# A gated linear recurrence and its MLP: decays of the states on ScalarE, block products for the last eight chunks, one mask operation per visit

## The chip, the cores and the metric

The kernel runs on one core of a Trainium2 chip. The metric is the device time of one execution in microseconds. Five engines with queues of their own work side by side: TensorE (PE in the profile; its weight loads are PEld), VectorE (DVE), ScalarE (ACT), GpSimd (POOL) and SyncE (SP), which issues the DMA transfers here. Every engine takes its instructions in order, so an instruction that waits holds up all behind it on that engine.

## What is computed

Four batches of eight heads run a recurrence over 768 tokens with a head width of 48. The state is a complex 48x48 matrix; each row is multiplied by a complex gate, whose magnitude is clipped at 0.999, and the outer product of key and value is added. The output of a token is the query times the real part of the new state. The heads' outputs form 3072 rows of 384, which run through an MLP: 384 to 2048 features, a leaky ReLU with a slope per feature, and back to 384.

```python
mag = np.sqrt(a_re * a_re + a_im * a_im)
scale = np.minimum(mag, 0.999) / (mag + 1e-06)
a_re_n, a_im_n = (a_re * scale, a_im * scale)
for t in range(S):
    ar, ai = (a_re_n[:, :, t, :, None], a_im_n[:, :, t, :, None])
    new_re = ar * S_re - ai * S_im
    new_im = ar * S_im + ai * S_re
    kv = np.einsum('bhd,bhe->bhde', k[:, :, t], v[:, :, t])
    S_re, S_im = (new_re + kv, new_im)
    y[:, :, t] = np.einsum('bhd,bhde->bhe', q[:, :, t], S_re)

x = np.ascontiguousarray(attn_out.transpose(0, 2, 1, 3)).reshape(B * S, H * D)
h = x @ w_in
g = np.maximum(h, 0.0) + alpha * np.minimum(h, 0.0)
return (g @ w_out).astype(np.float32)
```

## The kernel before, in words

The tokens are cut into 24 chunks of 128, six for each batch. A gate is split into a magnitude (the decay) and a rotation. The rotation is put into queries and keys, so that the state needs only real decays, one for each of the 96 rows (real and imaginary parts of 48) of each head.

**Gates** (`gates`, L223). A group of one or three chunks is worked through at once; the list `GATES` (L947) names the groups as (batch, first chunk, end). The large steps, over all tokens of a group, run on ScalarE and VectorE (L253 to L318, then L426 and L429 for the final rotations). Between them lies a long chain of dependent small steps that form running products of the rotations (`product`, L334 to L342; `three`, L363; L372 to L411). The names `tiny` and `small` decide which engine takes the small ones: VectorE in batch 0, GpSimd in the others (L232). The results go to DRAM (`decs`, `phs`) and are loaded back in another layout by `loads`, as PP and T. Two gate tiles are held at a time.

**Units** (`unit`, L637). One unit works a chunk through. L661 and L663 put the rotations on keys and queries. Then the positions inside the chunk are treated as a tree of six levels, 1, 2, 4, 8, 16 and 32, two levels in a "visit". For each level TensorE multiplies keys and queries (L678), the result in PSUM (`ps_lv`) is masked into a tile A of that level, and `step` (L717) multiplies queries and keys with the decays of that level on VectorE. Levels 1 to 8 are masked by VectorE, one operation each (L702), levels 16 and 32 by ScalarE (L699). Afterwards TensorE forms the chunk's own state terms (L797, tile `ps_kv`), the output from the levels (L817) and the output from the states before (L841), and the states go on: multiplied by the decay (L826) and added to (L829). The output is copied (L855) and goes through DRAM to become x of the MLP (`loads_x`).

**MLP** (`all_mlp`, L926). Groups of MLP rows are single chunks at both ends and pairs between (`sizes`). For each of the 16 blocks of 128 features, TensorE makes the features (`features`, L889: three matmuls into `ps_h`, two tiles of it), ScalarE and VectorE make the leaky ReLU (L896, L898), and `outputs` (L908) adds the block's product with w_out, 128 rows by 384 columns, to `ps_o`. After 16 blocks the sum is copied (L918) and sent. The output products of a group follow while the features of the next are made. The weights come in as 64-bit words and are turned into 32-bit floats at the start (`to_f32`: L507 to L511 on ScalarE, L515 on GpSimd, L517 and L519 on VectorE).

**Order.** Each of these routines is a generator; a `yield` stands ahead of each operation. The string `ORDER` names, letter by letter, which generator makes its next operation, and so fixes the order of the instructions on every engine and of the DMA issues. Waits follow from the data and the buffers: the `bufs` of each tile are what limits how far an engine may run ahead.

Of the kernel before, what the change touches and what calls it, by code (L numbers as in the profile page):

```python
# [9 lines left out]
F32 = mybir.dt.float32  # L10
# [8 lines left out]
P = 128  # L19
# [11 lines left out]
    "AABAMMAAAAAAAAAAAAAAAAAMAAAAAMABJMNAJNNABNAAAAAAAAAAAAANKJKAKBKNBAABAAAABABBJAAAALAAAAAAABAMAAAAOKAK"  # L31
    "AOBAAABMAAABAAABBBABLLBABAOMABAKBABABBBALNBNABABAABBOBAKBNBABBNOBNBOOOABBBOBMBBBNLONNBBBBBBOBLBBBOBN"
    "NOBBJBKJBNJBPBBBBBOBPBBPBBBPBCCBBOBKBPPPBNLBMPJCKBBCPLBLKKPBMBBOPKKOKBBCBPBCBPMBCBPBLPBNCLPLCPLBPBCP"
    "CLPCCCNPJJJCJONJNPCDCPPPPPPPPPPDPCPPCJMPCCPKPCPCQCQCNOCDPJCNCQCNLQCCPQJJCPCPQCDQPPNOPOCOQCOPJPCQPPPC"
    "DOQMCQNCQDLJQJnCQLQJCQCKKKLQDDQKOLCCKoQCKNONCQLLNCRCQNQCRQCQRNQDQQKCQMQODLCLRDQCRLNRRDDCLLORCQOLCQON"
    "ooCRCNCRLRMKOCCOCDONCJDQQMNDQCODNCRDCDRCCQNQOLCQCROCOMLRCLRMOCLODoDQJCLCCRQKRCCQCooLooLCLRQDLLLLLLCN"
    "QoRCDRDCDCoCKCCRCRCCCoRRRDoCKRRooRQCRCoCoooCJQQQRQooDRNoDoRRRQDJCRDRoNooooJooJoooRJoDoooORDooooooLLL"
    "LLLoooDODoDnoRDooRoOoERDRooNNRRLDoRoSRRoooNOoNooSoEooOoooNOSLOoSoNROSSoooSJDooSJJSJSLSJOooooooSSSooS"
    "SLSoDooELoLLSSooooooDSSLESoJSJoSSSSSooDooSSToDoooSDoSoETDEDTDoJoSSoSSJJSSEDoTSoooKJoTTooKooLDDoEoDoS"
    "LTKTToToDoDLSoLoDoTKoEEDTDSSoTTToSDDDLDoJLSoSSSooooSoDoDDEoooDToTToooDoEoLoooLDTnooDUoDLooEooooooEDo"  # L40
    "oEToTTDDDDDToToDJJJETJUooDoTDToooUoTTLLLEooLooooLToDUDETUTUUToETTTToUoDLDDoUDUDoUDTDoooooUooKDoKTLUo"
    "EUTUTTTEDDDLDoEEEoDoooooJJoDoTTKKoTToooELoooEDoooooTLUUDUULoLooLooLLoooooDoUDEUooEoETEoDooDoooooEooo"
    "LooLUUUUoEUUEoUEoLEEoooooUEUoEoUooEEooEUoooJoVUUUUJJUoJUEUVUUEoUUUUEEVJEEEFVoVooVoJoooooVVVoJUVUoooV"
    "oJFEoVVoJonoJooVWooVooWVVFoEFVLoooLoVEoLLLLLLVoooWLooooVoLWEEEEEEEEEEEEEEEoLooLoLoLKWoWVFJVEEVWJVVVo"
    "VooWooVVVoooVoWoVoKWWVoVJVVWoVVWWJEVVFEEEEEVEEJEEEWWVoLWooWoLoLLLLLEWLoEEXoFEKoLooEoWWWEFWXVWWFLWVEo"
    "LLVFLLooWVoooVVVVFJJJJEJoooWoooWEooWEWooWWWWEWEEWWEWWWEooWEWoLEXLWFoWFLoooLoXoLWoWoLoLoEoFooXXFXooFX"
    "oooooFELWLoLJXLJLoKoXXooLooFoooFoXoooooXXXFFXoooXXoXoooFFooFFXXoXLXXYooXFXFooXWJFXoXJooXnoXXYoYoooXX"
    "XooJJJoYFoFXFFoGXFXXFJLXXFYYFXFFXYXLXLXooGoLLLFXoooXooLJXooYoYLYFFoJJoooYoooGFoKYoFoFoooJYFFFYYZFGFo"
    "ZFFoFoYooJooYoYoooYooGooZoZFYYYYFYoFFFFYFJFJFFLoFooLoYoooYoJoLYYLooGoYLZLZYoooYoGYYYYFYFLZFLLZZGYFYY"
    "LFoYFZYYGYFLZFFFFFFZGFFFFFFaoYYoFoYoooooYYLLoZZZoLZoZnoLoZoooooooJFFLoLLLLZGJJJoJFoZFFFFZoKZGoZZFaFZ"  # L50
    "FooooooZZFZoKZoooFFooFooooZZooZZZZZZFZJZoZZGGZoZoZFooaZZZZooaGGaLoZGLoaaGJooLoooaaoLLLLaLJooJaJoLoaG"
    "ooooooLooooooaaooGabaooGooboooooaoGaboaLoHGHoGboooobGooboooGaaabaaaaGaabooKKGJoGaLLbbKoaoooaGGbboGoo"
    "GaoaaaaJaGaGoaKGaaHHaGaGaJGoGGGGoaGoJoaooaoKKooHoHHLooGcGoGoJbbGoGoocHoooooooLbboLLLGGGboJJJJobcoLoo"
    "oGooLoLGLocbbobooGGoooooocbcLLLbbbbbcnoboboHbGJcboobcoocooLLbbooobbcHGGbbbcbHoGoGGGGcLcGcGbGHLLLLobH"
    "HbGJHLLLGocobboobGLGGcGGGoccboooboooGoLGLGooHGoocccoGHocLdbdbbcocGoccGoJcGGooLLoocooHcGoHooGGoJKcGoJ"
    "JGGGGGGGHoooooocodcccccoHLLLLoLLoooLdooLoccGGGoHdoodooodLHdoIdoooooodJodoIoooooooLLLHHcocooooodLHooo"
    "oHooddccdooododHHdcodoJIoHHcHdddddddddHHHcoocoooKJccoHLooooooooodoooeJdHooJooondooddHHdHdHdJedoJdIdo"
    "dJddIddddoHooeoHodoJdHoooLedJJJeIeeeHeHoHooLeHoooLHIeooooooHJHeoooeLILeLHoLoLeooLIoLeeJfefofKooofHeo"
    "oooooLoooLoefefeofLeoooeIJeIILoeeooeoeHHHeHHHoHHHHHHHofeoJoIeoeeefeoefeeeIIefeeIJeooeoooIofeeooIeooo"
    "eoLLfffIfooHooooJofffIoIoooJLgJoggHLJHHHHHooooLLooooKHLoLoHoJLoLKLKLLLHgHHfggooIHHfooonffffoffHoooJf"  # L60
    "foHHofooKHHfoKfggHggoooIIIIoHooHoffffHfffffffHooLLHLHHLoLoooooHoHoIogHoooHoooIoIofHgooooooIoofIoIfLo"
    "HIIfLLLLLggggKoIoooooogJgooooIfoKgoooooLoggfgoLoohggIhggoooghogoIgoooJggoIohJooIJgggggggggJKgIIggJJI"
    "ghooIhLggoohohoLoogLJLohhoJhhooohhooooJooohhhioohIIoJoihoooIIooIihooiohnoooooooLIIILLohihihLhoohhhJo"
    "IhhoooLoohiJLLoLoLIIoiIIhIIIohIhILIioooIhhhhhhhhhLhJhoohIIIiiiIJIooLIIIoIhIIIIhhoojLhLooohooooooiiio"
    "iojLiooooJiJioJLLLojoIjoLoooLLLLLoooooooiIiIJIiijiIjiiiIooooIiiIoiooIjioIoooooIojIIIooIooooJioiiIjii"
    "ijoiiLiiLiLILiiiojoijooiIioLjiLjJIjILIoLoLojoooJoJjoooojoooooooJoooojoojjJojoojJoLooLoooookLoooojLko"
    "ookLojjjjokojoJkknJoJoookoojoookjoooojoooojjkkjjlojjokLkkkkjLLLLLLLLjLokooooookoookkoooooojokkkkkkkj"
# [933 lines left out]
```

## Time and profile before

The times of three runs are 837.02, 833.38 and 836.58 us, with a median of 836.58. The profiled execution took 836.36 us; its profile has a span of 834.6 us and a mean granted TensorE clock of 0.962.

| What | Busy us | Share of the span | Instructions |
|---|---|---|---|
| TensorE, matmuls | 695.8 | 83% | 11488 |
| VectorE | 651.7 | 78% | 1020 |
| ScalarE | 438.7 | 53% | 937 |
| GpSimd | 200.6 | 24% | 293 |

Every float32 matmul shows as two records, so a count of matmuls in the profile is halved for the number of instructions in the program. A group's row gives line, engine, operation, tile out <- tile in, shape out <- shape in and the count; then the busy time and the mean length in ns; then the idle time of the engine just before, and what ended it. A line of the timeline gives the start and the length in us. The row of slices gives each fortieth of the span as tenths of busy time. The "chain that ended last" follows the work back from the last instruction, always to what released it.

### The profile page before, as it was taken

What the parts mean: (1) busy time and instruction counts of PE and PEld (TensorE: products, weight loads), DVE (VectorE), ACT (ScalarE), POOL (GpSimd) and SP (SyncE); (2) the same over time, 40 slices, a digit from 0 to 9 for tenths busy, and PEclk for the clock granted to TensorE, in tenths of its full rate; (3) what the DMA queues carried; (4) which work ended last, traced back from release to release, by engine and by line L of the source; (5) the groups of instructions that cost most, each with busy time, mean ns of one, the idle gap of its engine ahead of it and who ended that gap; (6) DMA issues with size and microseconds to landing.
All of it is one profiled execution on the core that took longest, in us unless ns stands there. A gap on an engine that the chain in (4) does not pass through costs nothing.

```text
span 834.6 us, 26848 instructions
## 1 busy us (share of the span) xinstructions
PE 695.8 (83%) x11488; PEld 527.7 (63%) x11488; DVE 651.7 (78%) x1020; ACT 438.7 (53%) x937; POOL 200.6 (24%) x293
## 2 busy tenths in 40 slices
PE   0001435889998999899999999999999999999998
PEld 0001424667776777677777777777777777777776
DVE  5989999999997899889988988979767652644112
ACT  7758787467635665565657446644344342323221
POOL 5231222328603600360135103330341000000000
PEclk9999755899999999999999999999999999999999
DMA  6696977786478579737873586457834832511110
GB/s 195 189 280 157 274 170 227 217 220 175 100 222 209 145 171 248 186 88 197 233 194 77 158 259 159 115 143 216 210 99 118 202 70 61 136 34 43 35 30 10
DMA packets 194174, 130.91 MB, mean 157 GB/s; under 512 B 74120, under 2 KB 185864, under 8 KB 194056
## 3 DMA queue, kind: packets, MB, share of 16 engines
q1 hardware_dynamic: 194056, 129.20, 58.8%
q8 instruction: 90, 1.47, 0.7%
q14 instruction: 28, 0.23, 0.1%
HBM read 100.82 MB, written 35.71 MB: 164 GB/s over the span
## 4 chain that ended last, share of the span: by engine, by line
PE 53%; DVE 23%; DMA 12%; POOL 4%; issue 4%; ACT 4%; SPq 1%; DVEq 0%; ACTq 0%; POOLq 0%
PE ps_o L908 22%; PE ps_h L889 20%; DVE KQ L717 4%; DMA T<-decs 4%; PE ps_lv L678 4%; DVE gate L426 3%; DVE gate L338 2%; PE ps_y L817 2%; DMA phs<-gate 2%; PE ps_y L841 2%; PE ps_kv L797 2%; DVE gate L429 2%; DMA g_sb<-in_w_out_dram 1%; POOL gate L338 1%; DVE gate L340 1%
## 5 line engine op out<-in xcount | busy, mean ns | idle before, releaser
L889 PE MATMUL ps_h<-xT,w_in_sb 128*128 128x256 f32 (+1 forms) x1344 | 297.3, 355 | 9.0 <-DMA xT<-ysc 7.0
L908 PE MATMUL ps_o<-w_out_sb,g_sb 128*128 128x384 f32 x768 | 297.2, 500 | 7.9 <-DVE g_sb L898 4.5
L889 PEld LDWEIGHTS ps_h<-xT,w_in_sb 128*128 128x128 f32 x1344 | 235.7, 194 | 82.1 <-DMA xT<-ysc 7.8
L898 DVE SCALAR_TENSOR_TENSOR g_sb<-g_sb,al,ps_h 128x256 f32<-128x256 f32 (+1 forms) x224 | 97.5, 436 | 117.9 <-ACT g_sb L896 117.6
L896 ACT ACTIVATE g_sb<-ps_h 128x256 f32<-128x256 f32 (+1 forms) x224 | 78.8, 352 | 200.7 <-PE ps_h L889 199.4
L908 PEld LDWEIGHTS ps_o<-w_out_sb,g_sb 128*128 128x128 f32 x768 | 136.5, 191 | 59.4 <-DVE g_sb L898 7.0
L717 DVE TENSOR_TENSOR KQ<-KQ,T 96x1024 f32<-96x1024 f32 x120 | 149.2, 1246 | 23.8 <-PE ps_lv L678 15.2
L678 PE MATMUL ps_lv<-WQ 96*32 96x32 f32 x2304 | 34.3, 204 | 72.6 <-DVE WQ L661 56.2
L678 PEld LDWEIGHTS ps_lv<-WQ 96*32 96x32 f32 x2304 | 26.5, 116 | 92.7 <-DVE WQ L661 56.2
L740 ACT COPY WQ<-KQ 96x1024 f32<-96x1024 f32 x48 | 49.9, 1040 | 22.2 <-DVE KQ L717 22.2
L338 POOL TENSOR_TENSOR gate<-gate 128x72 f32<-128x72 f32 x42 | 25.8, 615 | 134.3 <-ACT gate L368 131.5
L515 POOL TENSOR_SCALAR top<-top 128x768 f32<-128x768 f32 x16 | 41.2, 2578 | 65.2 <-ACT top L507 65.1
L756 ACT COPY W<-KQ 96x512 f32<-96x512 f32 x48 | 30.9, 644 | 40.1 <-DVE KQ L717 30.3
L338 DVE TENSOR_TENSOR gate<-gate 128x576 f32<-128x576 f32 (+5 forms) x84 | 48.6, 579 | 3.8 <-ACT gate L368 2.4
L855 ACT COPY T<-ps_y 48x256 f32<-48x256 f32 x96 | 31.6, 365 | 34.5 <-PE ps_y L841 33.7
L817 PE MATMUL ps_y<-A,VL 64*48 64x64 f32 x2304 | 42.0, 224 | 4.4 <-issue 3.8
L426 DVE TENSOR_TENSOR gate<-gate 128x1152 f32<-128x1152 f32 (+2 forms) x36 | 43.6, 1235 | 0.1
L817 PEld LDWEIGHTS ps_y<-A,VL 64*48 64x48 f32 x2304 | 39.7, 125 | 5.4 <-issue 4.5
L699 ACT ACTIVATE A<-ps_lv,columns 128x64 f32<-128x64 f32 x144 | 37.6, 334 | 9.2 <-PE ps_lv L678 9.1
L678 PE MATMUL ps_lv<-KQ,W 96*32 96x32 f32 x1536 | 24.5, 203 | 20.3 <-ACT W L756 19.7
L702 DVE TENSOR_TENSOR A<-ps_lv,mask 128x256 f32<-128x256 f32 x96 | 37.6, 412 | 0.0
L717 DVE TENSOR_TENSOR KQ<-WQ,T 96x1024 f32<-96x1024 f32 x24 | 29.5, 1231 | 6.4 <-DMA T<-decs 4.2
(106 smaller groups left out, 899.4 us busy)
## 6 DMA issues: line engine op xcount, KB each, us to landing
T<-decs SPq DMA_DIRECT2D x48, 384.0 KB
PP<-phs SPq DMA_DIRECT2D x24, 387.0 KB
KQ<-in_q_dram SPq DMA_DIRECT2D x48, 192.0 KB
decs<-gate SPq DMA_DIRECT2D x7, 1152.0 KB
phs<-gate SPq DMA_DIRECT2D x14, 576.0 KB
KQ<-in_k_dram SPq DMA_DIRECT2D x40, 192.0 KB
vsc<-in_v_dram SPq DMA_DIRECT2D x48, 144.0 KB
VL<-vsc SPq DMA_DIRECT2D x24, 288.0 KB
```

Source lines behind the costliest of these rows:

```text
L338: on(4 * k).tensor_tensor(out=m, in0=w[:, 1::-1].unsqueeze(2).to_broadcast([P, 2, 2, k]), in1=pairs_of(u), op=ALU.mult)
L426: TT(out=m[:, a], in0=U5[:, 1 + a], in1=turned(off3, o)[:, a].unsqueeze(1).unsqueeze(3).to_broadcast([P, L // 2, nb, 2]), op=ALU.mult)
L515: nc.gpsimd.tensor_scalar(out=top, in0=top, scalar1=F64_SMALL, scalar2=None, op0=ALU.max)
L678: nc.tensor.matmul(t[64 * i + j:64 * i + j + HC // 2, p], lhsT=keys(n, g), rhs=queries(n, g), start=True, stop=True)
L699: nc.scalar.activation(a[:, :, cols], t[:, :, at:at + name], AF.Copy, scale=s)
L717: nc.vector.tensor_tensor(out=x, in0=x if x0 is None else x0, in1=m, op=ALU.mult)
L740: nc.scalar.copy(z.rearrange("p i n t -> p i (n t)").rearrange("p i (m h) -> p m i h", h=h), bass.AP(tensor=KQ.tensor, offset=KQ.offset + ...
L817: nc.tensor.matmul(o, lhsT=Vp[h][64 * i:64 * i + 64, s, e_ * D:(e_ + 1) * D], rhs=a, start=False, stop=False)
L889: nc.tensor.matmul(p, lhsT=w_in_sb[:, f // 2, kk, f % 2 * P:(f % 2 + 1) * P], rhs=x_of[m][:, kk], start=(kk == 0), stop=(kk == NK - 1))
L896: nc.scalar.activation(gt, p, AF.Relu, scale=-1.0)
L898: nc.vector.scalar_tensor_tensor(out=gt, in0=gt, scalar=al_1[:, f:f + 1], in1=p, op0=ALU.mult, op1=ALU.add)
L908: nc.tensor.matmul(sums[0], lhsT=gt[:, c * P:(c + 1) * P], rhs=w_out_sb[:, f], start=(f == 0), stop=(f == NF - 1))
```

## The change

It has five parts.

1. *States.* The product of a state and its decay (one VectorE operation of 96x384) becomes eight ScalarE operations of 96x48, each with its decays as a scale per partition. The sum stays on VectorE.
2. *Masks.* A visit's two levels are masked by one operation of VectorE (128x512) instead of two; this holds for levels 1, 2 and 4, 8. The tile of levels 1 and 2 has two buffers, that of 4 and 8 one.
3. *Gates.* The three groups of batch 0 become two groups of three chunks. The small steps of the first are on VectorE, those of all others on GpSimd.
4. *Output products of the last eight chunks.* Two chunks of rows, the features in two halves and the output columns in two halves make a product of 2x2 by 2x2 blocks. It is formed as seven block products with sums and differences of blocks in place of eight. The blocks of w_out are combined once (`more`), the rows' features per pair (`sides`, `fourth`), and the results are put together from PSUM (`plus`). The last two groups of one chunk form one such pair.
5. *Order and waits.* The string ORDER is another one throughout. Three PSUM tiles are allocated once and handed on through a list, and matmuls that write them, loads of KQ and loads of T are marked as having no dependency on one another, where another wait covers it.

```diff
-        tiny, tiny_engine = (DVE, nc.vector) if b == 0 else (POOL, nc.gpsimd)
+        tiny, tiny_engine = (DVE, nc.vector) if g == 0 else (POOL, nc.gpsimd)
...
-                e = yield DVE(HP * n, e, takes=(R[name],))
...
+        def mask_both(name, t, e):
+            e = yield DVE(2 * HP * HC, e, takes=(R[name],))
+            a = work.tile([P, 2, HP, HC], F32, tag=f"A{name}", name=f"A{name}", bufs=2 if name == 1 else 1)
+            k = LEVELS.index(name)
+            whole = [P, 2, HP, 2, HC // 2]
+            nc.vector.tensor_tensor(out=a.rearrange("p a n (g t) -> p a n g t", g=2), in0=t.unsqueeze(3).to_broadcast(whole),
+                                    in1=both_masks[:, k:k + 2].rearrange("p a (g t) -> p a g t", g=2).unsqueeze(2).to_broadcast(whole),
+                                    op=ALU.mult)
...
-            k_ = yield DVE(H * D, known, takes=(R["St"],))
-            St = work.tile([D2, H, D], F32, tag="St", name="St", bufs=3)
-            nc.vector.tensor_tensor(out=St, in0=before, in1=T[0:D2, :, TL - 4 + s:TL - 3 + s].to_broadcast([D2, H, D]),
-                                    op=ALU.mult)
+            for n in range(H):
+                if n % 4 == 0:
+                    k_ = yield ACT(4 * D + 300, known, takes=() if n else (R["St"],))
+                if n == 0:
+                    St = work.tile([D2, H, D], F32, tag="St", name="St", bufs=3)
+                nc.scalar.activation(St[:, n], before[:, n], AF.Copy, scale=T[0:D2, n, TL - 4 + s:TL - 3 + s])
             k_ = yield DVE(H * D, ek, k_)
             nc.vector.tensor_tensor(out=St, in0=St, in1=kv[s][0:D2], op=ALU.add)
...
+    def more():
...
+        held["T"] = [B11, T2, B12, T4, B21, T1, B22]
+        for dst, a, b in ((T1, B12, B11), (T2, B22, T1), (T4, B21, T2)):
+            for f in range(0, NH, 4):
...
+                nc.vector.tensor_tensor(out=dst[:, f:f + 4], in0=a[:, f:f + 4], in1=b[:, f:f + 4], op=ALU.subtract)
...
+            nc.vector.tensor_tensor(out=B12[:, f:f + 4], in0=B22[:, f:f + 4], in1=B12[:, f:f + 4], op=ALU.subtract)
...
+    def parts(m):
+        A = home(m)
+        A11, A12, A21, A22 = [A[:, r * NH:(r + 1) * NH, c] for c in range(2) for r in range(2)]
+        S1, S2 = held["S"]
+        held[m] = A11, S2, A21, A22, A12, S1, S2
+    def sides(m, r):
+        A11, S2, A21, A22, A12, S1, _ = held[m]
+        for dst, a, b, op in ((S1, A21, A22, ALU.add), (A21, A11, A21, ALU.subtract), (S2, S1, A11, ALU.subtract)):
+            for f in range(0, NH, 4):
+                r = yield DVE(4 * P, r)
+                nc.vector.tensor_tensor(out=dst[:, f:f + 4], in0=a[:, f:f + 4], in1=b[:, f:f + 4], op=op)
+        return r
...
+    def group(m, j, r, tag="o"):
+        for k in range(NH):
...
+            nc.tensor.matmul(z, lhsT=held[m][j][:, k], rhs=held["T"][j][:, k], start=k == 0, stop=k == NH - 1)
...
+    def plus(dst, z, u, *e, takes=()):
+        t = yield DVE(DH, *e, takes=takes)
+        nc.vector.scalar_tensor_tensor(out=dst, in0=z, scalar=scale, in1=u, op0=ALU.mult, op1=ALU.add)
+        return t
...
+    def product(m, made):
...
+        if alone:
+            yield from second()
+            yield "need", m + 1, NF - 1
+        r = yield from sides(m, made[m + alone, NF - 1][1])
...
-    GATES = [(0, 0, 1), (0, 1, 3), (0, 3, 6)] + [(b, c, c + 3) for b in range(1, B) for c in (0, 3)]
+    GATES = [(0, 0, 3), (0, 3, 6)] + [(b, c, c + 3) for b in range(1, B) for c in (0, 3)]
```

With these edits the lines shift; those that the prediction speaks of are, before and after: L661 and L674 (the first operation of a unit), L702 and L718 (mask), L717 and L735 (step), L826 and L851 (state times decay), L829 and L853 (state plus terms), L426 and L437 (rotations), L889 and L954 (features), L896 and L969, L898 and L971 (leaky ReLU), L908 and L988 (output products), L918 and L997 (their copies). L1058, the block products' matmuls, is new.

## The prediction

> **What bounds the kernel now.** First the slices of the span and the chain.
>
> ```profile
> span 834.6 us, 26848 instructions
> PE 695.8 (83%) x11488; PEld 527.7 (63%) x11488; DVE 651.7 (78%) x1020; ACT 438.7 (53%) x937; POOL 200.6 (24%) x293
> PE   0001435889998999899999999999999999999998
> DVE  5989999999997899889988988979767652644112
> PEclk9999755899999999999999999999999999999999
> PE 53%; DVE 23%; DMA 12%; POOL 4%; issue 4%; ACT 4%; SPq 1%; DVEq 0%; ACTq 0%; POOLq 0%
> ```
>
> Up to slice 13 VectorE is at 9 and TensorE idles and grows; from there TensorE is full to the end while VectorE thins out. So two stretches with two bounds. To find the border I read the start of chunk u on VectorE, its one L661 per chunk, in the timeline (chunks 0, 3, 6, 12), and the stretches between them:
>
> ```profile
> 54.91 1.21 DVE L661 TENSOR_TENSOR WQ<-KQ,PP 96x1024 f32<-96x1024 f32 x1
> 167.98 1.21 DVE L661 TENSOR_TENSOR WQ<-KQ,PP 96x1024 f32<-96x1024 f32 x1
> 400.95 1.21 DVE L661 TENSOR_TENSOR WQ<-KQ,PP 96x1024 f32<-96x1024 f32 x1
> ```
> ```profile
> core 0: us, PE busy (x) PEld busy (x) DVE busy (x) ACT busy (x) POOL busy (x), PEclk, DMA share, GB/s
> 56.00:168.00 112.00, 50.64 (x1266) 41.88 (x1267) 109.65 (x186) 82.16 (x135) 27.97 (x16) 0.76 0.79 214
> 248.00:401.00 153.00, 143.65 (x2627) 107.33 (x2618) 135.75 (x179) 86.73 (x186) 45.43 (x78) 0.99 0.71 180
> 401.00:831.00 430.00, 427.81 (x6307) 321.14 (x6305) 285.79 (x421) 182.78 (x446) 67.84 (x119) 1.00 0.47 124
> ```
>
> From 56 to 168 us VectorE is busy 109.65 of 112: what it has to do before chunk 3 is the time. From 401 us TensorE is busy 427.8 of 430. Hence: less VectorE work counts up to chunk 12, less TensorE work counts after it, and what lies past the last feature is added bare. The rows that price the change:
>
> ```profile
> L702 DVE TENSOR_TENSOR A<-ps_lv,mask 128x256 f32<-128x256 f32 x96 | 37.6, 412 | 0.0
> L826 DVE TENSOR_TENSOR St<-St,T 96x384 f32<-96x384 f32 x44 | 25.4, 577 | 0.4
> L699 ACT ACTIVATE A<-ps_lv,columns 128x64 f32<-128x64 f32 x96 | 23.6, 312 | 9.1 <-PE ps_lv L678 9.1
> L515 POOL TENSOR_SCALAR top<-top 128x768 f32<-128x768 f32 x16 | 41.2, 2578 | 65.2 <-ACT top L507 65.1
> 266.31 2.91 PE L889 MATMUL ps_h<-xT,w_in_sb 128*128 128x256 f32 x6 [2.12 <-DMA xT<-ysc]
> 270.04 1.46 PE L889 MATMUL ps_h<-xT,w_in_sb 128*128 128x256 f32 x6
> ```
>
> The sum is made against the profiled execution, 836.4 us (834.6 of span and 1.8 around it); the median shown is 836.6. Line numbers are those of before, L...a those of the changed kernel.
>
> **VectorE's work, chunk 0 to 3.** I counted each engine's instructions in the order that the two programs give it, with the durations of the trace (0.06 us less for each, as they overlap). Ahead of chunk 3's L661 stand 147.5 us before and 127.7 after. It comes from: the gates' small steps, 125 operations for 25.4 us become 52 for 11.9, because three groups of batch 0 become two and the second one's go to GpSimd (-13.5); the large gate steps 55.0 to 53.5; the tree of decays 6.0 to 5.0; states 5.9 to 2.0, where L826 is gone; masks 4.2 to 3.7; other parts, the weight conversions above all, move by under 1. The masks by rows: 256 elements take 0.412 and the 1024 of L717 take 1.246, so 512 take 0.69; 48 x 0.69 = 33 for 37.6. The counts ahead of chunk 0 are 37.0 and 49.0, as three chunks' gates and not one's must be ready. So chunk 0 starts later by 12, at 67 (the ScalarE steps and the first loads, three times as large, are in series there too; before, 18 us of waits lie ahead of chunk 0, and I keep them). From chunk 0 to 3 VectorE has 78.7 left instead of 110.5. To this I add 8 for waits (below): chunk 3 at 67 + 79 + 8 = 154, before 168: **-14**.
>
> **Chunk 3 to 12.** Work 209.7 before, in 233.0 us; after, 340.4 - 127.7 = 212.7, as part of the later gates moved in here. States and masks give 15 less here, the new places of gates and weights take them back. I let the waits fall by the same 3: chunk 12 at 387, still -14. TensorE's queue ahead of chunk 12 is 231.6 before and 231.7 after, so nothing is moved past the border.
>
> **What the small steps cost on GpSimd.** Group (0,3,6)'s chain now runs there. Six such chains of later groups (first L338 of 72 columns to L411) took 33.2, 39.2, 29.3, 35.9, 45.9 and 38.0 us. It can start near 91.5 and VectorE needs it at its L426 (L437a) near 124, so 33 fits and 41 is late by 8. GpSimd is in order: three L515 of the weights stand among its steps, and each waits for ScalarE's L507. Cover for a later end is none: behind L437a on VectorE stand chunk 3's steps. Bounds 0 and 14 (the 45.9 chain), taken 8.
>
> **The states on ScalarE.** 352 activations of 96x48 with a scale per partition. Nothing like them is in the trace; above, L699 (64 elements, scale per partition) runs six in 1.42, 0.237 each; below, L368 of 18 columns has a pace of 0.12. So 42 to 83 us, taken 70 (0.2), nearer the upper row as that one has the same kind of operand. ScalarE goes from 439 to about 500 of 820, 61%, so in mean it is covered. Chunk 0 to 3 is the tight place: 74 us of work in 87, 85%, against 81 in 112 before. A state takes 1.6 instead of 0.6 until L829 may add, and behind the eight activations wait L740 and L756, which the chunk's TensorE steps need; chunks stand 26 us apart there, so a us each is hidden: 0, up to 16 (third rival). The trace prices ScalarE's scaling as not much dearer for a whole tile than the 0.577 of L826: 8 x 0.2 = 1.6. The Trainium skill (ScalarE: Activation LUTs, Rules for kernel authors) says that plain multiplies belong on VectorE rather than ScalarE; that agrees with 1.6 for 0.577, but speaks of one operation and not of which engine is full. By the same page's costs (What ACT_TABLE_LOAD costs) I estimate a pace of 0.226, 80 us, which would make the total ScalarE share 62%.
>
> **Level tiles with one buffer less, waits dropped.** The mask of levels 4 and 8 has one buffer, so it waits for the previous chunk's L817. Levels 8, 16 and 32 have one already, and L699's idle (9.1) is all put to ps_lv, none to L817. Cost 0; at worst half a us in 24 chunks, 12. The dependencies that are dropped are on loads and PSUM tiles whose releaser is older; the "issue" of the chain is 4%, 33 us, and I take 0 of it. SP has seven transfers fewer (733 to 726), larger ones; its queue is 1% of the chain.
>
> **Block products.** Out go 128 matmuls of 384 columns, 0.646 each: 82.7. In come 224 of 192 columns. The paces 0.223, 0.432 and 0.646 for 128, 256 and 384 are linear, so 0.328: 73.5. Saved 9.2, all on TensorE where it is 99.5% busy; with issue gaps (434 us elapsed for 396 of counted work) at most 10.1, taken **-9.7**. VectorE gets 35 us for it (8 of 768 elements, 32 of 512, 28 of 192), in a stretch where it has 144 us free: hidden, but for the last group's.
>
> **The end.** Before, TensorE has a new output matmul between features to the last, and idles 0.74 there. After, the last group's features come without outputs in between: 13 cycles of 0.79 instead of 0.67, the h buffers waiting for ScalarE and VectorE (0.28 + 0.35), +1.5. Behind the last feature come 0.28, 0.35 and six sums of 512 elements (0.6, less than L338's 0.752 at 576) before the next product can start: 4.4 idle, of which 0.74 was there: +3.7. Then five products, 40 x 0.328 = 13.1. After an idle time of 2.12 the trace shows six records in 2.91 where they later take 1.46: half clock, and 3.4 us long, so 1.45 are lost. The Trainium skill (TensorE: Matmul & The Clock Gate, Part 1) tells the same, half rate until some 3.4 us have been busy; by it the loss would be an estimated 1.7. Sum **+6.6** (bounds: 2, if the order keeps other products for the gap, and 12, if the sums run behind other VectorE work).
>
> **Sum.** 836.4 - 14 - 9.7 + 6.6 = 819.3, so **819**.
>
> **Rivals.**
> - *VectorE's remaining waits go too.* From chunk 3 to 12 it idles 23 us of 233, mostly behind transfers (12% of the chain) and TensorE's levels. With fewer buffers shared and dropped dependencies 16 of them could go: 803. For it speaks that VectorE is again the bound there; against it, DMA is at 0.71 busy.
> - *ScalarE bounds the front.* It is in order, with 85% load from chunk 0 to 3. If it reaches only its 72% of before (81 in 112), the stretch lasts 74 / 0.72 = 103, 16 over my 87: 835, no change. Against it: on ScalarE the load was never the chain's end (4%).
> - *Slower: GpSimd's chain.* VectorE waits at L437a for group (0,3,6). With three L515 inside that wait their mean 4.1 (65.1 / 16) and take 2.58, a chain of 33 to 46 becomes 53 to 66. From 58 (25 late) the gain is gone; at 65 it is 33 late: 819 + 25 = 844. For it: POOL waits for ScalarE, and ScalarE is fuller now. Against it: later groups' chains had conversions nearby too, and held 46.
> - *The change doesn't do what it says*: the products' count is in the program, 224 for 128; only their pace could be off. At 0.36 the gain would be 2 instead of 9.2, and the time 826, inside the range.
>
> **Chances.** The sum 0.50, the first rival 0.20, ScalarE 0.15, GpSimd 0.15. A measurement of this kernel can tell about 0.5%, 832.4 to 840.8, from no change. Faster: the first two and a third of ScalarE's, 0.75; same: the rest of it, 0.10; slower 0.15. The range leaves out the outer half of the first rival and most of the last: 802 to 840. The likeliest case's own range is 810 to 828.
>
> **What would show it.** L674a (the chunk starts) at 67, 154 and 387; VectorE's idle ahead of L437a in group (0,3,6), released by GpSimd, 0 to 14; ScalarE under 90% between chunk 0 and 3; the activations at 0.2 apart; L718a near 0.69; L1058a at 0.328 a matmul; a gap near 4.4 on TensorE before the last 40 matmuls, with the clock at half behind it. Wrong it would be through a later start (ScalarE in series with nothing beside it), or if TensorE, given less in the middle, waits for features' x at the end of VectorE's stretch.

## The result and the profile after

The changed kernel takes 846.88 us (median of 841.65, 845.46, 848.3 and 850.7), the kernel before 836.21 in the runs beside it. The ratio is 1.011, with an interval of 1.0077 to 1.0144: it became about 1% slower, where 819 us and a gain of 2% had been forecast. The profile after is of the execution of 850.7 us, the slowest of the four. The median of the kernel before differs a little from one group of runs to the next (836.2 to 840.9), so the experiments below are compared by their ratio to the kernel before that ran beside them, and a difference of a few us between two medians of different groups says little.

First the page's totals, slices and chain of the changed kernel:

```profile
span 848.9 us, 27360 instructions
PE 695.1 (82%) x11680; PEld 554.4 (65%) x11680; DVE 648.4 (76%) x903; ACT 512.9 (60%) x1262; POOL 244.8 (29%) x329
PE   0001417789798989899999999999999999999997
DVE  4999978988797989789898796787859785743332
PEclk9999956999898999999999999999999999999999
PE 63%; DVE 13%; ACT 7%; POOL 6%; DMA 3%; issue 3%; SPq 3%; DVEq 0%; ACTq 0%; POOLq 0%
```

The engines have the work that was reckoned with, but VectorE's part of the chain went from 23% to 13%, and the slices of TensorE from the ninth to the seventeenth show eights and sevens, with dips of its clock beside them. The starts of chunk 0, 3 and 12 on VectorE (start, length), and the stretches between them, tell where the time went:

```profile
69.21 1.84 DVE L674 TENSOR_TENSOR WQ<-KQ,PP 96x1024 f32<-96x1024 f32 x1
162.81 1.21 DVE L674 TENSOR_TENSOR WQ<-KQ,PP 96x1024 f32<-96x1024 f32 x1
413.36 1.22 DVE L674 TENSOR_TENSOR WQ<-KQ,PP 96x1024 f32<-96x1024 f32 x1
```
```profile
core 0: us, PE busy (x) PEld busy (x) DVE busy (x) ACT busy (x) POOL busy (x), PEclk, DMA share, GB/s
69.00:163.00 94.00, 44.16 (x1084) 36.11 (x1084) 83.62 (x103) 73.16 (x146) 59.83 (x52) 0.80 0.74 216
163.00:413.00 250.00, 228.58 (x4165) 171.35 (x4165) 213.62 (x279) 172.62 (x447) 92.64 (x124) 0.95 0.67 174
```

The stretch from chunk 3 to 12 in the kernel before, in the same columns:

```profile
168.00:401.00 233.00, 217.18 (x3918) 164.66 (x3917) 213.36 (x294) 135.38 (x298) 80.47 (x122) 0.99 0.70 179
```

Chunk 0 starts 14 us later than before, chunk 3 is 5 earlier, as VectorE has less to do between them. Then chunk 3 to 12 takes 250.5 us instead of 233.0, with the very VectorE work that was counted (213.6 busy; 212.7 forecast). TensorE is busy for 228.6 of these 250 at a mean clock of 0.95; in the same stretch before it was 217.2 of 233 at 0.99. The loss lies there: at chunk 12 the kernel is 12 us behind the kernel before, where it was forecast 14 ahead. This execution missed the forecast by 31 us (850.7 for 819): 9 were missing at chunk 3, 17 more at chunk 12, and 5 behind it, where 435.5 us remain, 433.7 remained before and about 431 were forecast.

The rows of the new operations, by shape. The length in the row of L718 is what was forecast (0.679 us for 0.69). The rows of L851 and L1058 give the length of one record, which overlaps the next one; the paces that were forecast are the times from start to start. These are 0.225 us in the median for L851 (0.2 forecast) and 0.163 for a record of L1058, 0.326 for a matmul of two records (0.328 forecast).

```profile
L718 DVE TENSOR_TENSOR A<-ps_lv,masks 128x512 f32<-128x512 f32 x48 | 32.6, 679 | 0.0
L851 ACT ACTIVATE St<-St,T 96x48 f32<-96x48 f32 x352 | 85.6, 324 | 12.7 <-DVE St L853 11.5 <-DVE g_sb L971 1.1
L853 DVE TENSOR_TENSOR St<-St,ps_lv 96x384 f32<-96x384 f32 x20 | 11.0, 548 | 15.3 <-ACT St L851 15.3
L1058 PE MATMUL ps_o<-w_out_sb,gate 128*128 128x192 f32 x112 | 20.6, 327 | 0.0
```

What is new is TensorE's stops. The view of its waits from 160 us on (total, how often, longest), first of the changed kernel, then of the kernel before:

```profile
PE ps_misc L807 <- ACT T L810: 7.0, 2, 4.8
PE ps_o L988 <- issue: 5.2, 3, 2.3
PE ps_o L1058 <- DVE gate L1021: 3.8, 1, 3.8
PE ps_y L839 <- issue: 3.2, 1, 3.2
...
PE ps_h L954 <- issue: 2.3, 1, 2.3
```
```profile
PE ps_lv L678 <- ACT W L756: 4.0, 6, 2.2
PE ps_o L908 <- issue: 3.0, 1, 3.0
...
PE ps_h L889 <- issue: 1.3, 1, 1.3
PE ps_y L817 <- issue: 0.9, 1, 0.9
```

All such waits after 160 us add up to 30.8 us against 18.3. After most of the longer ones the granted clock falls to half for 3.4 or 6.8 us at a time. Summed from the records of the clock, TensorE runs at half clock for 30.1 us after the first 160, against 10.5 before; the last record of each trace, 2.8 and 3.7 us of these, lies behind TensorE's work.

**An account.** TensorE's matmuls at their full pace are 619.5 us of work now and 628.8 before (an estimate: the counts of each shape times its pace). Take from 160 us on TensorE's waits and half of its time at half clock: 30.8 + 15.1 = 45.9 now, 18.3 + 5.3 = 23.6 before. The difference, 22.3, less the 9.3 of work saved is 13.0; the two spans differ by 14.3. This sum also holds roughly for the experiments (table at the end of the next section), so I use it to read them: from 160 us on the time is TensorE's work, its stops, and the clock behind the stops. It is bookkeeping: it tells where the time lies, and not what caused a stop.

### The profile page after: what moved, and what is told of

Its sections match the earlier page's. It is cut to its first block, busy times and chain, and to the rows that moved or that the text cites. A ratio compares the mean times of both kernels' runs of the same rounds, so it can differ in the third digit from the quotient of the medians.

```text
span 848.9 us, 27360 instructions
## 1 busy us (share of the span) xinstructions
PE 695.1 (82%) x11680; PEld 554.4 (65%) x11680; DVE 648.4 (76%) x903; ACT 512.9 (60%) x1262; POOL 244.8 (29%) x329
## 4 chain that ended last, share of the span: by engine, by line
PE 63%; DVE 13%; ACT 7%; POOL 6%; DMA 3%; issue 3%; SPq 3%; DVEq 0%; ACTq 0%; POOLq 0%
PE ps_h L954 25%; PE ps_o L988 15%; PE ps_o L1058 8%; PE ps_lv L691 4%; PE ps_y L839 3%; DVE KQ L735 3%; PE ps_y L867 2%; PE ps_misc L819 2%; PE ps_misc L807 2%; ACT St L851 2%; POOL gate L349 1%; POOL gate L351 1%; DVE gate L437 1%; DMA PP<-phs 1%; POOL gate L410 1%
## 5 line engine op out<-in xcount | busy, mean ns | idle before, releaser
L954 PE MATMUL ps_h<-xT,w_in_sb 128*128 128x256 f32 (+1 forms) x1344 | 297.7, 357 | 3.1 <-issue 2.3
L954 PEld LDWEIGHTS ps_h<-xT,w_in_sb 128*128 128x128 f32 x1344 | 232.1, 193 | 56.2 <-DVE g_sb L971 2.1
L988 PE MATMUL ps_o<-w_out_sb,g_sb 128*128 128x384 f32 x512 | 204.8, 510 | 12.2 <-DVE g_sb L971 5.5
L735 DVE TENSOR_TENSOR KQ<-KQ,T 96x1024 f32<-96x1024 f32 x120 | 148.6, 1240 | 37.6 <-PE ps_lv L691 23.8
L969 ACT ACTIVATE g_sb<-ps_h 128x256 f32<-128x256 f32 (+1 forms) x176 | 63.7, 363 | 111.6 <-PE ps_h L954 110.7
L988 PEld LDWEIGHTS ps_o<-w_out_sb,g_sb 128*128 128x128 f32 x512 | 91.1, 193 | 49.5 <-issue 9.4
L971 DVE SCALAR_TENSOR_TENSOR g_sb<-g_sb,al,ps_h 128x256 f32<-128x256 f32 (+1 forms) x176 | 78.6, 449 | 56.8 <-ACT g_sb L969 56.3
L691 PE MATMUL ps_lv<-WQ 96*32 96x32 f32 x2304 | 34.5, 204 | 84.1 <-DVE WQ L674 71.1
L691 PEld LDWEIGHTS ps_lv<-WQ 96*32 96x32 f32 x2304 | 26.6, 116 | 104.1 <-DVE WQ L674 71.1
L851 ACT ACTIVATE St<-St,T 96x48 f32<-96x48 f32 x352 | 85.6, 324 | 12.7 <-DVE St L853 11.5
L349 POOL TENSOR_TENSOR gate<-gate 128x72 f32<-128x72 f32 x49 | 31.6, 645 | 175.8 <-ACT gate L379 172.6
L758 ACT COPY WQ<-KQ 96x1024 f32<-96x1024 f32 x48 | 50.0, 1041 | 23.8 <-DVE KQ L735 23.6
L969 ACT ACTIVATE gate<-ps_h 128x128 f32<-128x128 f32 (+1 forms) x48 | 15.0, 313 | 55.0 <-PE ps_h L954 54.9
L349 DVE TENSOR_TENSOR gate<-gate 128x576 f32<-128x576 f32 (+1 forms) x63 | 44.9, 713 | 1.2 <-ACT gate L321 0.2
L971 DVE SCALAR_TENSOR_TENSOR gate<-gate,al,ps_h 128x128 f32<-128x128 f32 (+1 forms) x48 | 18.6, 390 | 35.4 <-ACT gate L969 35.2
L839 PE MATMUL ps_y<-A,VL 64*48 64x64 f32 x2304 | 41.9, 225 | 4.1 <-issue 4.1
L839 PEld LDWEIGHTS ps_y<-A,VL 64*48 64x48 f32 x2304 | 40.0, 127 | 5.4 <-issue 5.1
L774 ACT COPY W<-KQ 96x512 f32<-96x512 f32 x48 | 30.7, 639 | 21.0 <-DVE KQ L735 17.7
L437 DVE TENSOR_TENSOR gate<-gate 128x1152 f32<-128x1152 f32 x32 | 42.8, 1371 | 0.5 <-POOL gate L422 0.4
L691 PE MATMUL ps_lv<-KQ,W 96*32 96x32 f32 x1536 | 24.4, 204 | 20.9 <-ACT W L774 20.9
```

Of the source, the lines that this page charges most:

```text
L349: on(4 * k).tensor_tensor(out=m, in0=w[:, 1::-1].unsqueeze(2).to_broadcast([P, 2, 2, k]), in1=pairs_of(u), op=ALU.mult)
L437: TT(out=m[:, a], in0=U5[:, 1 + a], in1=turned(off3, o)[:, a].unsqueeze(1).unsqueeze(3).to_broadcast([P, L // 2, nb, 2]), op=ALU.mult)
L691: turned(nc.tensor.matmul(t[64 * i + j:64 * i + j + HC // 2, p], lhsT=keys(n, g), rhs=queries(n, g), start=True, stop=True))
L735: nc.vector.tensor_tensor(out=x, in0=x if x0 is None else x0, in1=m, op=ALU.mult)
L758: nc.scalar.copy(z.rearrange("p i n t -> p i (n t)").rearrange("p i (m h) -> p m i h", h=h), bass.AP(tensor=KQ.tensor, offset=KQ.offset + ...
L839: nc.tensor.matmul(o, lhsT=Vp[h][64 * i:64 * i + 64, s, e_ * D:(e_ + 1) * D], rhs=a, start=False, stop=False)
```

## The experiments

Theories at the start. A: ScalarE's new work holds up its queue, and VectorE behind it. B: the new order costs, whichever engine has the states. Later ones: C, GpSimd is held up by VectorE and ScalarE hands that on; D, TensorE's stops of "issue" are its own instructions coming late.

### The states' products back on VectorE, and alone on ScalarE

```diff
--- e1_states_vector, from the changed kernel
-                nc.scalar.activation(St[:, n], before[:, n], AF.Copy, scale=T[0:D2, n, TL - 4 + s:TL - 3 + s])
+            nc.vector.tensor_tensor(out=St, in0=before, in1=T[0:D2, :, TL - 4 + s:TL - 3 + s].to_broadcast([D2, H, D]),
+                                    op=ALU.mult)
--- e2_before_states_scalar, from the kernel before: the other way round, at the same place in the order
```

> The changed kernel with the states' products back on VectorE, one operation just ahead of the sum; the order of all else is kept. Theory A (ScalarE): the eight operations hold up ScalarE's queue, and VectorE waits behind them at the sums (20.9 us of idle time ahead of L853, 10.5 ahead of L829 before). Then chunk 12 starts near 400 instead of 413 and the time is 835 to 840. Theory B (the order): the states' engine does not matter, VectorE has 25 us more to do, 12 of it before chunk 12, and the time is 847 to 855.

> The kernel before with one part of the change: the states' products as eight ScalarE operations, at the place in the order where VectorE had its one. Theory A: 843 to 850, as ScalarE's queue delays its copies and masks and VectorE waits for the sums. Theory B: 834 to 839, as ScalarE has 40% of its time free and VectorE gets 25 us back.

e1_states_vector takes 847.7 us, ratio 1.0106 (1.0072 to 1.0141): the same as the changed kernel. Chunk 12 starts at 406.6 instead of 413.4, but half of that is given back by chunk 20 (648.5 and 651.7), and the medians are level. e2_before_states_scalar takes 866.14, ratio 1.0343 (1.0303 to 1.0383), 29 us slower, more than theory A had for it. VectorE's waits over the whole span, first of e2_before_states_scalar, then of the kernel before:

```profile
DVE St L829 <- ACT St L827: 52.7, 31, 4.0
```
```profile
DVE St L829 <- PE ps_kv L797: 8.8, 7, 2.7
```

Both theories are half right. Eight operations on ScalarE in an order that was made for one on VectorE cost 29 us, as VectorE's sums wait for them 31 times. In the new order, which places them, the engine makes no difference that these runs can tell (about 3 us). So the move is neither the gain nor the loss here.

### The end of the kernel

```diff
--- e3_tail, from the changed kernel
+        if alone:
+            z3, e3 = yield from group(m, 3, made[m + 1, NF - 1][1], lv)
+            r = yield from sides(m, made[m + 1, NF - 1][1])
+            z5, e5 = yield from group(m, 5, r, lv)
+            z, e = yield from group(m, 1, [t1, r], o)
...
```

> The changed kernel with the last group's block products in another order: the product that needs no sums runs right behind the last feature, then the one that needs the first sum only. If the end loses what the trace shows, 3.85 us of idle TensorE and 3.4 us of half clock behind it, the gap closes and the time falls by 4 to 6, to 841 to 843. If VectorE's sums behind the last feature set the end whatever TensorE does, it falls by 0 to 2.

It takes 842.76, ratio 1.0077 (1.005 to 1.0104), 4 us less by the medians, as expected; the traces differ by 8.5, in which other stops are shorter, too. The two intervals overlap a little, but the same edit takes 4.3 us off e10_scalar_no_wait and 6.3 off e12_shift_240 (both below), and the trace shows the step itself. The product after the last feature in the changed kernel, and what is left of the gap in e3_tail (the timeline, with the idle time before in brackets):

```profile
830.20 1.68 PE L1058 MATMUL ps_o<-gate 128*128 128x192 f32 x7 [3.85 <-DVE gate L1021]
```
```profile
833.74 1.08 PE L1058 MATMUL ps_lv<-w_out_sb,gate 128*128 128x192 f32 x5 [1.10 <-DVE top L1066]
```

### The block products

```diff
--- e4_plain_outputs, from the changed kernel
-        queue = [[m, product(m, made), None, None] for m in range(FIRST, LAST + 1)]
+        queue = []
...
+        for j in jobs:
+            yield from outputs(*j, *made[j[0::2]])
--- e6_before_products: the kernel before with more(), product() and the rest, the end as in e3_tail
--- e7_before_products_masks: with mask_both as well
```

> The changed kernel without block products: the last eight chunks get their output products as before (128 matmuls of 384 columns), placed by the features they stood beside; the rest of the order is kept. If the block products save their 9.2 us less the loss at the end (5 to 6), the time rises by 3 to 4, to 850. If their sums on VectorE and their PSUM tiles cost more than that on the way, it falls below 846.

> The kernel before with the block products alone (the last group's in the order of e3_tail), the letters of all else in their old order. If the products' gain does not hang on the new order: 837 less 9.2 less what the old end idled, plus the features without outputs, 826 to 830. If the 35 us of sums on VectorE need the new order to find room: 834 or more.

> e6_before_products with one mask operation per visit, too, issued at the second one's place. VectorE has 5 us less, 2 of it before chunk 12: 0 to 3 us below e6_before_products; if TensorE's levels come later to VectorE for it, up to 3 above.

e4_plain_outputs takes 855.2, ratio 1.0205 (1.0172 to 1.0239), 8 us more than the changed kernel: the block products are worth 8 in their own order, more than the 3 that the prediction left them. e6_before_products takes 885.04, ratio 1.0545 (1.0484 to 1.0605): the same products, put into the old order, cost 44 against the kernel before beside them. SyncE's waits in it:

```profile
SPq L1073 <- DVE top L1068: 109.7, 8, 29.6
SPq L615 <- PE ps_lv L823: 58.1, 7, 22.2
```

SyncE waits up to 29.6 us at one store of results, in order, with the loads of later chunks behind it; TensorE's waits add up to 62.0. I put that down to how I placed the letters, and not to the products; no run shows it. e7_before_products_masks, 885.42, ratio 1.0503 (1.0445 to 1.0562), shows no difference by the masks. Neither tells what the products could give in an order made for them.

### GpSimd and ScalarE

In the changed kernel's trace the two longest stops behind ScalarE go back to GpSimd. In the timelines of GpSimd, ScalarE and TensorE:

```profile
210.25 6.72 POOL L410 TENSOR_TENSOR gate<-gate 128x126 f32<-128x126 f32 x1
217.80 0.42 POOL L410 TENSOR_TENSOR gate<-gate 128x126 f32<-128x126 f32 x1
```
```profile
218.25 0.44 ACT L416 ACTIVATE gate<-gate 128x288 f32<-128x288 f32 x1 [4.97 <-POOL gate L410]
220.56 0.34 ACT L810 COPY T<-ps_misc 128x128 f32<-128x128 f32 x1
```
```profile
220.96 0.90 PE L807 MATMUL ps_misc<-ident,KQ 96*128 96x96 f32 x4 [4.80 <-ACT T L810]
```

VectorE's operations around the end of the long one:

```profile
215.48 1.21 DVE L735 TENSOR_TENSOR KQ<-WQ,T 96x1024 f32<-96x1024 f32 x1
219.30 0.35 DVE L971 SCALAR_TENSOR_TENSOR g_sb<-g_sb,al,ps_h 128x128 f32<-128x128 f32 x1 [2.61 <-ACT g_sb L969]
```

The same GpSimd operation takes 0.42 or 6.72 us. During the 6.72 VectorE was 96% busy, mostly with operations that read two tiles in SBUF; the long operation ended 0.28 us after the last of them, and the short one ran while VectorE stood still. ScalarE's L416 waits for it, the copies L809 and L810 stand behind L416, and TensorE needs them.

```diff
--- e5_offsets_vector, from the changed kernel (L407 and L410, both o)
-            tiny_engine.tensor_tensor(out=m, in0=blk[:, :, 0:Rn - 1],
+            nc.vector.tensor_tensor(out=m, in0=blk[:, :, 0:Rn - 1],
...
-            tiny_engine.tensor_tensor(out=offv[:, o, 1:Rn], in0=m[:, 0], in1=m[:, 1], op=ALU.add)
+            nc.vector.tensor_tensor(out=offv[:, o, 1:Rn], in0=m[:, 0], in1=m[:, 1], op=ALU.add)
--- e10_scalar_no_wait, from the changed kernel, for all groups but the first (L424 and L429 likewise)
-        nc.scalar.activation(n2, off, AF.Square)
+            nc.gpsimd.tensor_tensor(out=n2, in0=off, in1=off, op=ALU.mult)
--- e11_tail_no_wait: e10_scalar_no_wait and e3_tail together
```

> The changed kernel with four of each group's small gate operations (L407 and L410, 252 and 126 columns) on VectorE instead of GpSimd, from the second group on. In the trace two of them took 6.72 and 5.32 us where the same form takes 0.42 and 0.67 at best, while VectorE was 96 to 100% busy; ScalarE's next gate step waited behind them, and TensorE stood still for 4.8 and 2.2 us with half clock behind it. Theory C (GpSimd is held up by VectorE, and ScalarE's queue hands it on): these two stops go and the time falls by 6 to 10, to 837 to 841. Rival: VectorE now waits in its own queue for GpSimd's chain, and the time is 846 or more.

> The changed kernel with three of each group's last small gate steps (L416, L424 and the copy at L429) on GpSimd instead of ScalarE, from the second group on, so that ScalarE's queue no longer waits there for GpSimd. Theory C2: TensorE's stops at the second transposes of a chunk (L807, 4.79 and 2.22 us in the trace, behind ScalarE's copies L809 and L810, which stand behind L416) go, with the half clock behind them (10 us of it, 5 lost): 836 to 842. Rival: ScalarE waits at another place, or the stops come at the next chunk, as with four operations on VectorE: 845 to 849.

> e10_scalar_no_wait and e3_tail together. If the time from 160 us on is TensorE's work, its stops and half the time at half clock, both gains add: 4 for the end as measured, and what e10_scalar_no_wait gains; 832 to 838 by theory C2, 841 to 845 by its rival.

Theory C fell as a way to the lost time. e5_offsets_vector takes 847.55, ratio 1.0077 (1.0044 to 1.0109): the stops at L807 shrink from 4.8 and 2.2 to 3.0 and 1.8, chunk 12 starts 6.5 us earlier, and chunk 23 starts within 1 us of where it did (722.6 and 723.3). e10_scalar_no_wait removes them all but for 0.7 us and takes 852.47, ratio 1.0174 (1.0107 to 1.0241), slower than either theory had it: after 160 us TensorE waits 6.2 us at L994 behind the leaky ReLU (3.0 at this place, L988, in the changed kernel) and 5.3 at L697 behind ScalarE's copies (0.9 at L691). e11_tail_no_wait, 848.17, ratio 1.0119 (1.0087 to 1.0151), is the better by the end's 4 us, and no faster than e3_tail alone.

### The dropped waits

```diff
--- e8_all_waits, from the changed kernel
-        tc.add_to_no_dep_group("load", i.ins)
+        pass
...
-        tc.declare_no_dep(i.ins, group="load", reason="the engine that this waits for has written all of it since")
+        pass
```

> The changed kernel with the marks taken off that drop dependencies of loads and PSUM tiles; instructions and order are the same. By the prediction's step the dropped waits are worth 0: 845 to 848. If they are worth what the issue time of the chain is, it is 10 or more slower.

It takes 864.71, ratio 1.0292 (1.0241 to 1.0342), about 15 us slower than the changed kernel by the ratios, with the same matmuls, loads of weights and other operations in the same order. What grew is TensorE's "issue" (12.5 to 19.8 us) and its half clock (30.1 to 47.2). TensorE's queue has 188 waiting instructions of their own instead of 158, which also moves all later instructions; the next experiment shows what such a move does, so the waits' own price stays open.

### Where TensorE's instructions lie

The stops of "issue" come after the same few records in the kernels with the same TensorE instructions (2478, 5274, 8071, 10869 and 14681 among them; not every kernel stops at each), whatever the time. TensorE's instructions are loaded by a queue of their own, in blocks of 16 KB:

```profile
q8 instruction: 92, 1.51, 0.7%
```

23360 records and 161 waits and drains of TensorE fill 92 such blocks at 256 instructions each. Counted with the waits, every stop of "issue" over 0.5 us after 160 us, in both kernels, lies at 193 plus a multiple of 256 (2497, 3521, 5313, 8129, 10945, 14785 and 20673 in the changed one; 4545, 6593, 8385 and 16833 before), give or take one, and a block's load began 2.3 to 3.0 us before the work went on. In the traces of all 18 kernels of this document it is the same: 136 such stops, each at 193 or 194 plus a multiple of 256, with a load that began 2.2 to 3.1 us before. Which block a load brings is not in the trace; that it is the one that TensorE waits for is my reading. One of each, from the timeline of TensorE, the changed kernel first:

```profile
167.25 0.32 PE L839 MATMUL ps_y<-A,VL 64*48 64x64 f32 x7
170.78 0.48 PE L839 MATMUL ps_y<-A,VL 64*48 64x64 f32 x17 [3.20 <-issue]
```
```profile
336.61 0.81 PE L908 MATMUL ps_o<-w_out_sb,g_sb 128*128 128x384 f32 x2 [2.97 <-issue]
```

```diff
--- e9_shift (64), e12_shift_240 (120), e13_tail_shift_240 (120, on e3_tail); e14_before_shift_88 (44) and e15_before_shift_148 (74) on the kernel before
+        for _ in range(64):
+            nc.tensor.matmul(misc.rearrange("p n d -> p (n d)")[0:D, 0:2 * P], lhsT=nothing[0:64], rhs=ident.bitcast(BF16)[0:64],
+                             start=True, stop=True)
         plan.run(ORDER)
```

These matmuls of zeros run while TensorE has nothing to do for 60 us. They only move the rest of its instructions against the blocks.

> The changed kernel with 64 matmuls of zeros (two instructions each) ahead of everything, where TensorE has nothing to do for 60 us. Theory D: the stops of TensorE put down to issue (after record 2478, 5274, 8071, 10869 and 14681, the same records in four kernels whatever the time) are late loads of its instruction blocks of 16 KB, one of which the trace shows landing at each of them. Then they belong to places in the instruction stream: 128 instructions more, half a block of 64-byte instructions, make them come some 128 records of the old program earlier, at other matmuls, or go away and come up elsewhere; the time moves by up to 8 us either way. Rival: they come from what the instructions there wait for, and stay at the same matmuls of the program.

> The changed kernel with 120 matmuls of zeros (240 instructions) ahead of everything. In all runs so far, blocks of 256 TensorE instructions that were used up in under 4 us were followed by a stop in 50 to 78% of the cases (1.0 to 1.6 us in mean), those of over 6 us never. By these shares the blocks' ends of the changed kernel cost 8.6 us as it stands, 16.4 with 128 instructions more and 4.8 with 240. Theory D: the stops for issue fall from 12.5 to 5 to 8, half clock with them: 837 to 842. Rival (128 instructions cost 18 us for another reason, such as their being there at all): 855 or more.

> e3_tail with the same 240 instructions. Theory D: 4 below e12_shift_240, 833 to 838; if so, the changed kernel less two accidents is level with the kernel before.

> The kernel before with 44 matmuls of zeros (88 instructions) ahead of everything, the place where by the same shares its blocks' ends cost most, 21.7 us in place of the 6.0 measured. Theory D: the kernel before gets slower by 12 to 20 with no change of its work, to 849 to 857. Rival: the kernel before has no such stops whatever the place, 835 to 840.

> The kernel before with 74 matmuls of zeros (148 instructions), the place where its blocks' ends cost least by the shares, 5.8 us; as it stands it had 6.0. Theory D: 834 to 839, the same. Rival (the added matmuls themselves cost): above 842.

e9_shift takes 864.92, ratio 1.031 (1.025 to 1.037), 18 us slower, more than the 8 that I had allowed. Its stops of "issue" go from 12.5 to 22.0 us, and lie at other places, nearly all in the short matmuls of L839. Its waits of TensorE after 160 us, and one place of the timeline:

```profile
PE ps_y L839 <- issue: 20.7, 11, 3.9
```
```profile
326.51 0.88 PE L839 MATMUL ps_y<-A,VL 64*48 64x64 f32 x48
330.03 0.55 PE L839 MATMUL ps_y<-A,VL 64*48 64x64 f32 x24 [2.64 <-issue]
```

The kernel before does the same: e14_before_shift_88 takes 863.31, ratio 1.0325 (1.0287 to 1.0363), and e15_before_shift_148 takes 868.72, ratio 1.0395 (1.0357 to 1.0433). The waits of e15_before_shift_148:

```profile
PE ps_y L817 <- issue: 23.2, 14, 3.8
PE ps_y L841 <- issue: 7.4, 3, 4.0
```

Both are more than was expected. The added matmuls themselves do not cost it: in e15 they are done after 17.6 us, chunk 0 starts at 54.8 as before (54.9), and after 160 us the stops of "issue" grow by 27 us. So theory D holds, and my reckoning of the good places did not: I had put e15 at the best one. It went by how long a block lasted; what counts is where it ends. Over all 18 traces after 160 us, a block's end within 96 instructions of TensorE's queue of the end of a chunk's L817 (L839) matmuls stops TensorE in 132 of 285 cases, for 1.7 us in mean; further away in 17 of 1210. 96 of those matmuls take 1.3 to 1.5 us with as many weight loads, so a block of 256 is used up in under 2, and its successor needs the 2.2 to 3.1. e12_shift_240 has 5.9 us of "issue" instead of 12.5 and takes 845.07, ratio 1.0074 (1.0034 to 1.0113), above the 837 to 842 expected, and its interval does not separate it from the changed kernel. With the end mended, e13_tail_shift_240 takes 838.76, ratio 1.001 (0.9978 to 1.0042), level with the kernel before; the interval of e3_tail, which has the same end without the shift, lies above it (1.005 to 1.0104).

```diff
--- e16_tail_shift_vector: e13_tail_shift_240 with the edit of e1_states_vector
```

> e13_tail_shift_240 with the states' products back on VectorE. In the changed kernel this step moved the median by 1 us and TensorE's stops and half clock by 4. If ScalarE's queue was what the stops hid: 831 to 836, below the kernel before. If the order was made for either engine alike: 837 to 841, level.

It takes 837.26, ratio 0.9988 (0.9964 to 1.0011): level again. No version found beats the kernel before.

The account, in us, for the profiled executions. Each row is one execution; the four of the changed kernel alone differ by 9 us, and the one here is the slowest, so small differences between rows mean nothing. "Account" is waits plus half of the half clock, all after 160 us, less the 9.3 of work saved where the block products are in, against the same of the kernel before; "span" is the difference measured.

| Kernel | TensorE's waits | of these issue | half clock | account | span |
|---|---|---|---|---|---|
| before | 18.3 | 6.0 | 10.5 | 0 | 0 |
| changed | 30.8 | 12.5 | 30.1 | +13.0 | +14.3 |
| e1 states on VectorE | 28.6 | 10.8 | 26.1 | +8.8 | +11.7 |
| e2 before, states on ScalarE | 36.5 | 5.6 | 16.1 | +21.0 | +26.3 |
| e3 end | 26.2 | 11.3 | 23.1 | +4.9 | +5.8 |
| e4 plain products | 29.0 | 11.4 | 24.6 | +17.7 | +19.7 |
| e5 offsets on VectorE | 29.8 | 10.6 | 36.4 | +15.2 | +14.3 |
| e6 before, products | 62.0 | 17.8 | 50.3 | +54.3 | +57.6 |
| e7 before, products, masks | 57.6 | 17.4 | 43.2 | +46.4 | +48.6 |
| e8 all waits | 38.3 | 19.8 | 47.2 | +29.0 | +30.5 |
| e9 shift | 43.2 | 22.0 | 24.4 | +22.5 | +29.0 |
| e10 ScalarE without wait | 33.6 | 12.7 | 27.3 | +14.4 | +16.4 |
| e11 end, ScalarE without wait | 27.6 | 11.4 | 18.9 | +4.2 | +7.5 |
| e12 shift 240 | 24.6 | 5.9 | 19.3 | +1.4 | +3.7 |
| e13 end and shift | 22.8 | 7.2 | 26.2 | +3.0 | +4.5 |
| e14 before, shift 88 | 37.8 | 28.0 | 20.4 | +24.4 | +26.9 |
| e15 before, shift 148 | 42.5 | 32.9 | 32.5 | +35.2 | +36.7 |
| e16 end, shift, states on VectorE | 20.0 | 6.1 | 16.4 | -4.7 | -0.9 |

## Why the prediction was wrong

**The step that failed** is "Chunk 3 to 12", where the prediction let VectorE's work set the time and wrote "I let the waits fall by the same 3". The work was right (212.7 forecast, 213.6 busy), the elapsed time was 250.5 and not 233; VectorE stood still for 36 us of it, where it did so for 20 before and 20 were forecast. VectorE's work had been the bound to chunk 3; after that its total no longer sets the time. e1 shows it: with the states' products back on VectorE, which is more work for it, the stretch takes 243.6 us and not 250.5, and VectorE stands still for 17. That TensorE's stops set it instead is read from a count of its time, and no run changes them alone in this stretch. By this count the 17.5 us that the stretch is longer than before are 8.5 of half clock (11.9 lost now, 3.4 before), 5.6 of stops (21.1 and 15.5) and some 3.5 of work that had been done ahead of chunk 3 before. The longest of the stops are "issue" (9.0 in this stretch) and those at L807 behind ScalarE's copies (7.0). The prediction had no term for either: it took 0 for the "issue" of the chain, as a gain, and reckoned the clock for the end alone. Over the whole stretch from 160 us on, the stops of "issue" are 12.5 us for 6.0, by the runs a matter of placement, and the time at half clock 30.1 for 10.5. Why the stops at L807 fall where they do stays open, as e5 and e10 moved them and did not win the time.

- *Chunk 0* at 67: it was 69.2. *Chunk 3* at 154: it was 162.8. VectorE was busy for 83.6 of the 94 us and not for 78.7, and waited for 10.4 instead of 8.
- *GpSimd's chain* for group (0,3,6) ran from 99.0 to 139.2, in 40.2 us, 15 later than the 124 that was forecast for VectorE's need, but VectorE itself came to its L437 only at 141.2 and did not wait there: the slower rival did not come about. Slower came from another side.
- *The states on ScalarE*: eight in 1.90 to 1.92 us where nothing stands between them, a pace of 0.225 for 0.2, so that a state takes 1.9 us where one VectorE operation took 0.577, which is more than the "not much dearer" of the prediction; ScalarE was at 78% from chunk 0 to 3 (85% forecast) and 60% in all (61%). The waits at the sums are 23 us for 10.5, which the sum had at 0. It was right that ScalarE has room in total. The Trainium skill (ScalarE: Activation LUTs, Rules for kernel authors) would have the multiplies on VectorE; in the old order leaving them there is worth 29 us (e2), in the new one nothing that can be told (e1, e16).
- *Masks* 0.679 for 0.69; *block products* 0.326 for 0.328 a matmul, 9.3 saved for 9.2. The net of products and end was forecast at -3.1 and measured by e4 at -8.
- *The end*: 3.85 us of idle time for 4.4, and half clock for 3.4 behind it; e3 gave 4 back. The Trainium skill (TensorE: Matmul & The Clock Gate, Part 1) has the half rate last until some 3.4 us have been busy; in the trace it lasts 3.4 us or twice that. The prediction reckoned with it once, though each of the changed kernel's six stops of over 2 us after 160 us had half clock behind it. It is not so for every stop: one of 2.97 us in the kernel before, at 336.6, and some in the experiments (3.11 us in e8) left the clock full.
- *The dropped waits*, put at 0: e8 measures about 15, with the placement mixed in.

What stays open: how much of the 10 us is the accident of placement. With the end mended and the blocks moved, the ratio went from 1.011 to 1.001, but the best placement of each kernel is not known, and an order is not something that can be undone alone. Nor does any run bring the forecast gain: with end and placement mended chunk 12 still starts at 411.0 (e13) and 406.0 (e16), where 387 was forecast and the kernel before has 401.0.

## What to carry to other kernels

Find the engine that is the bound in each stretch, and then list its stops one by one: here most stops of TensorE of over 2 us cost themselves and half of the 3.4 or 6.8 us of half clock behind them. This small sum, made after the runs, gave the span of most versions within 3 us (6.5 at worst), while the forecast from counts of another engine's work missed by 28. An edit inside an order that was planned by hand is not one term: the same eight operations cost 29 us or nothing, the same products 44 us or minus 8. And before a change of under 3% is believed, shift the instruction stream: 88 to 148 instructions of nothing made either kernel 18 to 30 us slower, and 240 made the changed one no slower.

## What the hardware showed

**Instruction blocks.** Behind the bursts of short matmuls of each chunk TensorE stops, in about half of the cases where a block of 256 of its instructions ends there, for up to 4.2 us; I read it as waiting for the next block. The Trainium skill (Runtime: NRT & Kernel Launch, Instruction fetch mechanics) has blocks of 16 KiB and 256 instructions, as the trace shows here, and calls the crossing "mostly hidden". In these runs it is hidden at nearly all block ends among long matmuls, and not behind the short ones: the stops are 6 to 33 us of some 840 to 870, in kernels whose other work is the same.

**GpSimd beside VectorE.** An operation of GpSimd of 0.42 us took 6.72 while VectorE was busy, mostly with operations on two tiles in SBUF. The changed kernel's trace has 28 operations of the two shapes concerned (L407 and L410) on GpSimd. The eight that ran while VectorE stood still took 0.42 to 0.43 us (126 columns) or 0.67 to 0.68 (252); the thirteen that took over 1 us all ran beside a VectorE that was busy for 72% of the time or more; seven ran beside a busy VectorE and were short. The Trainium skill (SBUF — State Buffer, SBUF: two separate sides) says that the two share a pair of ports, held for a whole instruction; the long spans agree with that.
